# One-token attention over 16 heads on one core: the loads of K and V in another order, two K loads cut in two, and the bookkeeping of a turn moved

## The chip, the core and the metric

The kernel runs on one core of a Trainium2 chip. The core has five engines with queues of their own: PE (TensorE, matrix products; its weight loads are shown as PEld), DVE (VectorE), ACT (ScalarE), POOL (GpSimd) and SP (SyncE, which here only issues transfers). Sixteen DMA engines move data between the chip's main memory and the core's own. The metric is the time of one execution on the device, in microseconds (us).

## The reference

```
B, H, Sq, Sk, D = 1, 16, 1, 8192, 256            # bfloat16
scores = jnp.einsum("bhqd,bhkd->bhqk", q, k) * D ** -0.5
p = _softmax(scores, axis=-1)
return jnp.einsum("bhqk,bhkd->bhqd", p, v)
```

For each of 16 heads there is one query row. It meets 8192 rows of K, the 8192 scores go through a softmax, and the result weighs 8192 rows of V. K and V together are 134 MB, and each byte is used once.

## The kernel before, in words

**Tiling.** The 8192 rows of a head lie on 128 partitions, 64 rows on each: "column" j means the j-th row of each partition, 256 numbers long. One load brings all 64 columns of one head's K or V, 4 MB. K(h) goes to half h mod 2 of `kbuf`, V(h) to `vbuf[h % 2]`, so there are two buffers for each.

**Loads.** SP issues all loads in the order of the string `ORDER`, on one queue. K(h), from h = 2 on, waits until the maximum `m` of head h-2 is done, since then its buffer is free; V(h) waits until PE has finished the products of head h-2 (semaphore `pr`). SP takes its list strictly in order: a load that waits holds all those behind it. A few loads are cut by columns (`V_CUTS`), so that work on the first columns can begin before the rest has landed.

**A turn** is the work for one head's scores. For 24 of the 64 columns POOL multiplies K with q (`prod`, L171, six instructions of four columns each) and ACT sums each of them up (L360). For the other 40 columns DVE does both in one instruction each (L192), in five chunks of eight. All 64 sums per partition are in `S`. Then:

- DVE takes the maximum over the columns (`m`, L207), PE transposes it (L225), DVE takes the maximum over partitions (`g`, L209), PE broadcasts it (L227), ACT negates it (`negb`, L320) and takes the exponential (`E`, L323), whose sum over the columns is `lsum`.
- PE adds `lsum` over the partitions (`total`, L231), and DVE takes the reciprocal (L184).
- PE multiplies the weights `E` with V, two columns at a time in two strips (`doubles`, L238, 32 instructions per head), into the rows of `acc`. ACT copies four part rows of it into `comb` (`collect`, L336), PE adds them up with a selector (`gather`, L250), and ACT scales the row by the reciprocal (`final`, L342).
- The q row of the head after next is cast by PE (L215) and copied by ACT (`q_now`, L314).

The products with V run two heads behind the scores, the collecting and scaling three and four heads behind.

**The order on the engines** is that of the program text: each engine runs a hardware loop over the heads. On PE the turn h is: total of head h-1, products of head h-2, transposed maximum, broadcast, q row, gather. ACT's turn is: exponential of head h-1, six groups of four sums with `q_now` and `final` after the second group, and `collect` at the end. ACT's `collect` in a turn waits for PE's gather of the same turn (`pv`), and the exponential of the next turn stands behind it on ACT's queue.

**The end.** The last head's V lands in six pieces. The first 44 columns go by pairs, the other 20 singly into a row of their own, `ob_last` (L297). After ten of them the last total and the last gather come in.

Of the kernel before, what the change touches and what calls it, by code (L numbers as in the profile page):

```python
# [21 lines left out]
AHEAD = {"k1": 16, "sp": 2, "pr": 2, "cm": 3, "pv": 4, "fin": 4, "rc": 4, "l": 1, "ex": 1, "bc": 1, "nb": 1}  # L22
STREAM_AHEAD = ("v0", "v1", "v0_1", "v1_1", "v1_2")


def bass_standalone__mha_softmax__decode_kernel(nc: bass.Bass, q: bass.AP, k: bass.AP, v: bass.AP, out: bass.AP):
# [17 lines left out]
    def load(kind, h):  # L44
        cuts = (V_CUTS.get(h, (0,)) if kind == "v" else (0,)) + (J,)
        for n, (a, b) in enumerate(zip(cuts, cuts[1:])):
            stream.append((kind, h, a, b, f"{kind}{h % 2}" + (f"_{n}" if n else "")))
# [4 lines left out]
    with contextlib.ExitStack() as ctx:  # L52

        def sb(name, shape, d):
            return ctx.enter_context(nc.sbuf_tensor(name, shape, d))
# [25 lines left out]
        E = sb("E", [P, 2 * EW], BF16)  # L81
        comb = sb("comb", [ROWS, 2 * D], FP32)
        sel = sb("sel", [ROWS, 2], FP32)
# [29 lines left out]
        @(lambda f: f(nc.sync))  # L113
        def _(sp):
            for kind, h, a, b, name in stream:
                if h >= 2 and a == 0:
                    sp.wait_ge(sem("m"), h - 1) if kind == "k" else sp.wait_ge(sem("pr"), h + 1)
                buf = kbuf[:, h % 2 * J * D :] if kind == "k" else vbuf[h % 2]
                sp.dma_start(buf[:, a * D : b * D], src(k if kind == "k" else v, h)[:, a * D : b * D]).then_inc(
                    sem(name), 16  # L120
                )
# [13 lines left out]
        def _(pool):  # L135
# [29 lines left out]
            with pool.Fori(0, H) as h:  # L165
                par = pool.snap(h % 2)
                with pool.Fori(0, NG // 2) as i:
                    k_waits(pool, h)
                    for b in range(2):
                        pool.wait_ge(sem("sp"), h * NG + i * 2 + (b + 1))  # L170
                        pool.tensor_tensor(  # L171
                            out=prod[:, b * GRP * D : (b + 1) * GRP * D].rearrange("p (b d) -> p b d", b=GRP),
                            in0=kbuf[:, ds(par * (J * D) + i * (2 * GRP * D) + (JD + b * GRP) * D, GRP * D)].rearrange(
                                "p (b d) -> p b d", b=GRP
# [6 lines left out]
        def _(dve):  # L181
# [4 lines left out]
            with dve.Fori(0, H) as h:  # L186
                par = dve.snap(h % 2)
                with dve.Fori(0, NC) as c:
                    k_waits(dve, h)
                    for b in range(CH):  # L190
                        col = kbuf[:, ds(par * (J * D) + c * (CH * D) + b * D, D)]
                        ins = dve.scalar_tensor_tensor(  # L192
# [5 lines left out]
                            op1=ALU.mult,  # L198
                            accum_out=S[:, ds(h * J + c * CH + b, 1)],
# [9 lines left out]
                dve.tensor_reduce(g[:, :], mx[0:1, 0:P], AX.X, ALU.max).then_inc(sem("g"), 1)  # L209
            recips(LAST, 0)  # L210

        @(lambda f: f(nc.tensor))
        def _(pe):
# [8 lines left out]

            def maximum(h):
                pe.wait_ge(sem("m"), h + 1)
                pe.matmul(mx[0:1, 0:P], lhsT=m[:, :], rhs=ident[:, :], start=True, stop=True).then_inc(sem("mT"), 1)  # L225
                pe.wait_ge(sem("g"), h + 1)
                pe.matmul(sm, lhsT=ones_row[:, :], rhs=g[:, :], start=True, stop=True).then_inc(sem("bc"), 1)  # L227

            def total(h):
                pe.wait_ge(sem("ex"), h + 1)  # L230
                pe.matmul(tot[0:1, :], lhsT=lsum[:, :], rhs=ones_col[:, :], start=True, stop=True).then_inc(sem("l"), 1)  # L231

# [14 lines left out]

            def gather(dst, first, last):
                for n in range(2):
                    ins = pe.matmul(  # L250
                        dst[0:1, 0:D],
                        lhsT=sel[:, n : n + 1],
                        rhs=comb[:, n * D : (n + 1) * D],
                        start=first and n == 0,
                        stop=last and n == 1,
# [6 lines left out]
            for n in range(2):  # L262
                qcast(n, slice(n, n + 1))
            pe.wait_ge(sem("cf"), 4)
            with pe.Fori(0, H + 2) as h:
                par = pe.snap(h % 2)
                here = pe.snap(h // 2 * 16 + 16)
                late = pe.snap(h // H * 16 + 16)
                with pe.If(h > 0):
                    with pe.If(h < H):  # L270
                        total(h)
                with pe.If(h > 1):
                    with pe.If(par == 0):
                        doubles(0, 0, J, {0: (sem("v0"), here), HALF: (sem("v0_1"), late)}).then_inc(sem("pr"), 1)
                    with pe.If(par == 1):
                        cuts = V_CUTS[LAST]
                        waits = {b: (sem(f"v1_{n}"), late) for n, b in enumerate(cuts) if 0 < b < LAST_PAIRED}
                        doubles(1, 0, LAST_PAIRED, {0: (sem("v1"), here)} | waits)
                        with pe.If(h < H + 1):
                            doubles(1, LAST_PAIRED, J, {}).then_inc(sem("pr"), 1)  # L280
                with pe.If(h < H):
                    maximum(h)
                    qcast(par, ds(h + 2, 1))
                with pe.If(h > 2):
                    pe.wait_ge(sem("cm"), h + 1)
                    pe.wait_ge(sem("fin"), h + 1)
                    gather(ob, True, True).then_inc(sem("pv"), 1)
            for j in range(LAST_PAIRED, J):
                if j in cuts:
                    n = cuts.index(j)  # L290
                    pe.wait_ge(sem(f"v1_{n}"), 32 if f"v1_{n}" in STREAM_AHEAD else 16)
                if j == LAST_PAIRED + GATHER_AFTER:
                    total(H)
                    pe.wait_ge(sem("cm"), H + 3)
                    gather(ob_last, False, False)
                at = EW + j % 2 * HALF + j // 2
# [3 lines left out]
                    rhs=vbuf[1][:, j * D : (j + 1) * D],  # L300
                    start=(j == LAST_PAIRED),
                    stop=(j == J - 1),
                    skip_group_check=True,
                )
                if j == LAST_PAIRED:
                    ins.then_inc(sem("pr"), 1)
            ins.then_inc(sem("pv"), 1)

        @(lambda f: f(nc.scalar))
        def _(act):  # L310
# [21 lines left out]
            def collect(h, n):  # L332
                act.wait_ge(sem("pr"), h - n + 3)
                act.wait_ge(sem("pv"), h - n + 4)
                at = back(h, n) % 2 * (2 * D)
                act.activation(out=comb[:, :], in_=acc[0:ROWS, ds(at, 2 * D)], func=ACT.Copy).then_inc(sem("cm"), 1)  # L336

# [13 lines left out]
            q_copy(0)  # L351
            with act.Fori(0, H) as h:
                with act.If(h > 0):
                    expo(h, 1)
                with act.Fori(0, NG // 2) as i:
                    for n in range(2):
                        act.wait_ge(sem("tp"), h * NG + i * 2 + (n + 1))
                        for b in range(GRP):
                            part = prod[:, (n * GRP + b) * D : (n * GRP + b + 1) * D]
                            ins = act.activation(  # L360
                                out=part,
                                in_=part,
                                func=ACT.Copy,
                                scale=SCALE,
                                accum_out=S[:, ds(h * J + i * (2 * GRP) + (JD + n * GRP + b), 1)],
                            )
                        ins.then_inc(sem("sp"), 1)
# [6 lines left out]
            expo(H - 1, 0)  # L374
            final(H - 4, 0)
            collect(H - 2, 0)
            final(H - 3, 0)
            collect(H - 1, 0)
            final(H - 2, 0)
            final(H - 1, 0, ob_last)  # L380
            act.nop()
# [28 lines left out]
```

## Time and profile before

| what | value |
|---|---|
| median of 3 runs | 321.34 us (321.33 to 321.76) |
| the profiled execution's own time | 321.44 us |
| its span, first to last instruction | 319.8 us |
| mean granted TensorE clock | 0.733 of full speed |
| busy: PE / DVE / ACT / POOL | 42% / 73% / 60% / 64% of the span |
| DMA | 134.26 MB, 420 GB/s over the span |

Busy shares of engines are averages over the whole span. The DMA row of the 40 slices and the chain of the work that ended last say more here: the chain is followed back from the last instruction, at each step to what released it. An SP row is a transfer's issue; "DMA kbuf<-in_k_dram" in the chain is the time from issue to landing. Dates are us from the span's start.

### The profile page before, as it was taken

The numbers are of one execution on the slowest core, as the hardware profiler recorded it, in microseconds if no ns is written. First come the engines' busy times: TensorE is split into PE (matmuls) and PEld (weight loads), VectorE is DVE, ScalarE is ACT, GpSimd is POOL, SyncE is SP. The second block draws the span as 40 slices with busy tenths as digits, with TensorE's granted clock in tenths as the row PEclk, the third lists the DMA queues.
The fourth block names the chain that finished last, engine by engine and source line by source line (L and its number), as shares of the span: only waits on it lengthen the run. The fifth ranks groups of instructions, "written<-read, shape, count | busy, mean of one in ns | idle before, by whom it ended". The sixth has DMA issues, their size and how long they took to land.

```text
span 319.8 us, 7090 instructions
## 1 busy us (share of the span) xinstructions
PE 135.7 (42%) x700; PEld 54.2 (17%) x700; DVE 234.8 (73%) x1328; ACT 192.6 (60%) x866; POOL 203.7 (64%) x112
## 2 busy tenths in 40 slices
PE   0001017070554627264463523646526072370796
PEld 0000003030221212021121211212112030120343
DVE  0296979879795959779595978969695885949700
ACT  2085848666374857757484866747485773757631
POOL 2299785676594893939578575858484874929500
PEclk9999999758575775758576595755758568586799
DMA  8999999999999999999999999999999999999994
GB/s 329 434 418 459 393 455 434 422 451 402 455 422 365 434 418 447 422 439 447 410 447 422 439 434 422 447 410 451 426 430 443 410 451 422 434 434 414 428 410 162
DMA packets 5510, 134.26 MB, mean 420 GB/s; under 512 B 626, under 2 KB 643, under 8 KB 1284
## 3 DMA queue, kind: packets, MB, share of 16 engines
q1 hardware_dynamic: 5476, 134.23, 98.0%
q8 instruction: 1, 0.02, 0.0%
q10 hardware_dynamic: 32, 0.01, 0.0%
q14 instruction: 1, 0.01, 0.0%
HBM read 134.23 MB, written 0.01 MB: 420 GB/s over the span
## 4 chain that ended last, share of the span: by engine, by line
DMA 28%; POOL 23%; issue 13%; PE 12%; DVE 7%; ACT 7%; POOLq 4%; DVEq 3%; ACTq 3%; SPq 0%
POOL prod L171 23%; DMA kbuf<-in_k_dram 14%; DMA vbuf<-in_v_dram 13%; ACT prod L360 6%; DVE kbuf L192 5%; PE ob L250 5%; PE acc L238 2%; PE mx L225 2%; DVEq L192 2%; POOLq L171 2%; PE mx L227 1%; ACTq L360 1%; DVE m L207 1%; DVE g L209 1%; PE ob_last L297 1%
## 5 line engine op out<-in xcount | busy, mean ns | idle before, releaser
L171 POOL TENSOR_TENSOR prod<-kbuf,q_now 128x1024 f32 x96 | 201.8, 2123 | 94.5 <-DMA kbuf<-in_k_dram 46.6
L192 DVE SCALAR_TENSOR_TENSOR kbuf<-kbuf,qrow x640 | 225.0, 417 | 43.8 <-DMA kbuf<-in_k_dram 24.7
L360 ACT ACTIVATE prod<-prod 128x256 f32<-128x256 f32 x384 | 154.7, 404 | 48.3 <-POOL prod L171 48.3
L238 PE MATMUL acc<-vbuf,E 128*64 128x512 bf16 x502 | 86.7, 520 | 44.6 <-DMA vbuf<-in_v_dram 41.6
L360 ACT ACTIVATION_READ_ACCUMULATOR prod<-prod x384 | 71.7, 187 | 0.0
L192 DVE DVE_READ_ACCUMULATOR kbuf<-kbuf,qrow x640 | 52.8, 82 | 0.0
L238 PEld LDWEIGHTS acc<-vbuf,E 128*64 128x64 bf16 x502 | 37.1, 147 | 88.9 <-DMA vbuf<-in_v_dram 43.3
L225 PE MATMUL mx<-ident,m 128*1 128x128 f32 x32 | 8.3, 357 | 102.3 <-DVE m L207 102.1
L336 ACT ACTIVATE comb<-acc 97x512 f32 (+1 forms) x16 | 9.5, 596 | 58.2 <-PE ob L250 54.4
L250 PE MATMUL ob<-comb,sel 97*1 97x256 f32 x60 | 22.9, 524 | 0.4
L225 PEld LDWEIGHTS mx<-ident,m 128*1 128x1 f32 x32 | 1.4, 81 | 109.6 <-DVE m L207 109.6
L207 DVE TENSOR_REDUCE m<-S 128x1 f32 x16 | 3.5, 220 | 15.4 <-ACT prod L360 14.6
L231 PE MATMUL mx<-ones_col,lsum 128*1 128x1 f32 x32 | 3.0, 164 | 23.5 <-ACT E L323 23.5
L209 DVE TENSOR_REDUCE g<-mx 1x1 f32<-1x128 f32 x16 | 4.5, 278 | 9.8 <-PE mx L225 9.8
L184 DVE RECIPROCAL recip<-mx 1x1 f32 (+1 forms) x16 | 2.4, 151 | 12.6 <-PE mx L231 12.6
L323 ACT ACTIVATE E<-S,negb (+1 forms) x16 | 9.3, 580 | 3.9 <-ACT negb L320 3.9
L227 PE MATMUL mx<-g,ones_row 1*128 1x1 f32 x32 | 8.5, 332 | 5.9 <-DVE g L209 5.9
L227 PEld LDWEIGHTS mx<-g,ones_row 1*128 1x128 f32 x32 | 7.1, 276 | 12.9 <-DVE g L209 12.9
L215 PE MATMUL qrow<-q_sb,identb 16*128 16x256 bf16 x18 | 6.1, 350 | 5.7 <-DMA q_sb<-in_q_dram 5.7
L314 ACT ACTIVATE q_now<-qrow (+1 forms) x17 | 6.1, 362 | 3.7 <-PE qrow L215 3.7
L320 ACT ACTIVATE negb<-mx 128x1 f32<-128x1 f32 x16 | 2.6, 165 | 8.7 <-PE mx L227 8.7
L231 PEld LDWEIGHTS mx<-ones_col,lsum 128*1 128x1 f32 x32 | 1.5, 81 | 34.3 <-ACT E L323 34.3
(23 smaller groups left out, 30.3 us busy)
## 6 DMA issues: line engine op xcount, KB each, us to landing
kbuf<-in_k_dram SPq DMA_DIRECT2D x16, 4096.0 KB, 17.4
vbuf<-in_v_dram SPq DMA_DIRECT2D x14, 4096.0 KB, 25.9
vbuf<-in_v_dram SPq DMA_DIRECT2D x2, 2048.0 KB, 20.1
vbuf<-in_v_dram SPq DMA_DIRECT2D x1, 1536.0 KB, 8.2
vbuf<-in_v_dram SPq DMA_DIRECT2D x1, 768.0 KB, 10.5
vbuf<-in_v_dram SPq DMA_DIRECT2D x1, 640.0 KB, 11.6
vbuf<-in_v_dram SPq DMA_DIRECT2D x1, 512.0 KB, 9.1
vbuf<-in_v_dram SPq DMA_DIRECT2D x1, 384.0 KB, 12.1
```

What stands on the lines that cost most here:

```text
L171: pool.tensor_tensor(out=prod[:, b * GRP * D : (b + 1) * GRP * D].rearrange("p (b d) -> p b d", b=GRP), in0=kbuf[:, ds(par * (J * D) + i * ...
L192: ins = dve.scalar_tensor_tensor(out=col, in0=col, scalar=SCALE, in1=qrow[:, ds(par * 512, D)], op0=ALU.mult, op1=ALU.mult, accum_out=S[:, ...
L207: dve.tensor_reduce(m[:, :], S[:, ds(h * J, J)], AX.X, ALU.max).then_inc(sem("m"), 1)
L209: dve.tensor_reduce(g[:, :], mx[0:1, 0:P], AX.X, ALU.max).then_inc(sem("g"), 1)
L215: pe.matmul(qrow[:, ds(at * 512, D)], lhsT=identb[0:H, col].to_broadcast([H, P]), rhs=q_sb[:, :], start=True, stop=True,).then_inc(sem("qp ...
L225: pe.matmul(mx[0:1, 0:P], lhsT=m[:, :], rhs=ident[:, :], start=True, stop=True).then_inc(sem("mT"), 1)
L227: pe.matmul(sm, lhsT=ones_row[:, :], rhs=g[:, :], start=True, stop=True).then_inc(sem("bc"), 1)
L238: ins = pe.matmul(acc[at : at + STRIP, par * 2 * D : (par + 1) * 2 * D], lhsT=E[:, par * EW + j // 2 :][:, 0:STRIP], rhs=vbuf[par][:, j * ...
L250: ins = pe.matmul(dst[0:1, 0:D], lhsT=sel[:, n : n + 1], rhs=comb[:, n * D : (n + 1) * D], start=first and n == 0, stop=last and n == 1, s ...
L323: act.activation(out=E[:, ds(i % 2 * EW, J)].rearrange("p (two x) -> p x two", two=2), in_=S[:, ds(i * J, J)].rearrange("p (x two) -> p x ...
L336: act.activation(out=comb[:, :], in_=acc[0:ROWS, ds(at, 2 * D)], func=ACT.Copy).then_inc(sem("cm"), 1)
L360: ins = act.activation(out=part, in_=part, func=ACT.Copy, scale=SCALE, accum_out=S[:, ds(h * J + i * (2 * GRP) + (JD + n * GRP + b), 1)],)
```

## The change

It has six parts.

1. **Order of loads**: V0 and V1 stand ahead of K2, and V4 ahead of K6; K6 and K7 stand next to each other.
2. **K5 and K15 in two pieces**, columns 0 to 33 and 34 to 63. The second piece has a semaphore of its own (`k1_1`), on which DVE waits before each chunk with a computed value.
3. **GpSimd's 24 columns are the first of a head**, DVE's 40 the last, in four chunks of ten. The reciprocal moves from behind the fourth chunk to behind the second.
4. **Bookkeeping on ACT**: one loop over 19 turns. The part rows (`collect`) of head h-3 are copied at the beginning of turn h, then come the exponential, `final` and the q row, and then the six groups. `comb` has two halves.
5. **Bookkeeping on PE**: the gather stands between the transposed maximum and the broadcast, in each turn; the total is taken in each turn, and the last one ahead of the last gathers.
6. **The end**: 32 columns by pairs, the last 32 singly, added to the row that the last gather begins.

```
-CH = 8
+CH = 10
-V_CUTS = {14: (0, 32), 15: (0, 24, 32, 44, 54, 60)}
-LAST_PAIRED = 44
-GATHER_AFTER = 10
+CUTS = {"k5": (0, 34), "k15": (0, 34), "v14": (0, 32), "v15": (0, 24, 32, 44, 54, 60)}
-ORDER = "k0 k1 v0 k2 v1 k3 v2 k4 v3 k5 k6 v4 k7 v5 k8 ..."
+ORDER = "k0 k1 v0 v1 k2 k3 v2 k4 v3 k5 v4 k6 k7 v5 k8 ..."
+LAST_PAIRED = 32
...
 # SP
-sp.wait_ge(sem("m"), h - 1) if kind == "k" else sp.wait_ge(sem("pr"), h + 1)
+sp.wait_ge(sem("m"), h - 1) if kind == "k" else sp.wait_ge(sem("pr"), h + 2)
...
 # POOL
+pool.memset(lsum[:, :], 0.0).then_inc(sem("cf"), 1)
+pool.memset(comb[:, :], 0.0).then_inc(sem("cf"), 1)
...
 # DVE
+dve.wait_ge(sem("k1_1"), (h * 8 + c + 39) // 80 * 16 + 16)
 for b in range(CH):
-    col = kbuf[:, ds(par * (J * D) + c * (CH * D) + b * D, D)]
+    col = kbuf[:, ds(par * (J * D) + c * (CH * D) + (NPL + b) * D, D)]
...
-with dve.If(c == 3):
+with dve.If(c == 1):
     with dve.If(h > 0):
         recips(h, 1)
...
 # PE, in the loop
 with pe.If(h < H):
-    maximum(h)
-    qcast(par, ds(h + 2, 1))
-with pe.If(h > 2):
-    pe.wait_ge(sem("cm"), h + 1)
-    pe.wait_ge(sem("fin"), h + 1)
-    gather(ob, True, True).then_inc(sem("pv"), 1)
+    pe.wait_ge(sem("m"), h + 1)
+    pe.matmul(mx[0:1, 0:P], lhsT=m[:, :], rhs=ident[:, :], ...).then_inc(sem("mT"), 1)
+pe.wait_ge(sem("cm"), h + 1)
+pe.wait_ge(sem("fin"), h + 1)
+gather(ob, 1 - par, True).then_inc(sem("pv"), 1)
+with pe.If(h < H):
+    pe.wait_ge(sem("g"), h + 1)
+    pe.matmul(sm, lhsT=ones_row[:, :], rhs=g[:, :], ...).then_inc(sem("bc"), 1)
+    qcast(par, ds(h + 2, 1))
...
 # ACT
-with act.Fori(0, H) as h:
-    with act.If(h > 0):
-        expo(h, 1)
-    with act.Fori(0, NG // 2) as i:
-        ...
-        with act.If(i == 0):
-            q_copy(h + 1)
-            with act.If(h > 3):
-                final(h, 4)
-    with act.If(h > 1):
-        collect(h, 2)
+with act.Fori(0, H + 3) as h:
+    with act.If(h > 2):
+        collect(h, 3)
+    with act.If(h > 0):
+        with act.If(h < H + 1):
+            expo(h, 1)
+    with act.If(h > 3):
+        final(h, 4)
+    with act.If(h < H):
+        q_copy(h + 1)
+        with act.Fori(0, NG // 2) as i:
+            ...
```

Three places of the built programs show what moved. The first is SP's queue at its beginning; kbuf and vbuf are the buffers of K and V, `m` a head's maximum, `pr` the products with V. Of the change:

```order
L119 DMA kbuf<-in_k_dram 128x16384 [waits barrier_Pool_Activation_PE_DVE_SP_release]
L119 DMA kbuf<-in_k_dram 128x16384
L119 DMA vbuf<-in_v_dram 128x16384 x2
L119 DMA kbuf<-in_k_dram 128x16384 [waits m] x2
L119 DMA vbuf<-in_v_dram 128x16384 [waits pr]
L119 DMA kbuf<-in_k_dram 128x16384 [waits m]
L119 DMA vbuf<-in_v_dram 128x16384 [waits pr]
L119 DMA kbuf<-in_k_dram 128x8704 [waits m]
L119 DMA kbuf<-in_k_dram 128x7680
L119 DMA vbuf<-in_v_dram 128x16384 [waits pr]
L119 DMA kbuf<-in_k_dram 128x16384 [waits m] x2
```

Before, K2 with its wait stood between V0 and V1, and K5 and K6 followed each other; now the two V loads without a wait come first, K2 and K3 follow each other, and K6 and K7 do.

The second place is PE's turn behind the products: mx holds the transposed maximum, ob the gathered row, comb the part rows. Before:

```order
L225 MATMUL mx<-ident,m 1x128 [waits m]
L227 MATMUL mx<-g,ones_row 128x1 [waits g]
L215 ISA
L215 REGISTER_ALU
L215 MATMUL qrow<-q_sb,identb 128x256
L281 UNCONDITIONAL_BRANCH
L284 COMPARE_AND_BRANCH
L285 REGISTER_ALU
L250 MATMUL ob<-comb,sel 1x256 [waits fin,cm]
L250 MATMUL ob<-comb,sel 1x256
```

Of the change, at the same place:

```order
L281 MATMUL mx<-ident,m 1x128 [waits m]
L279 UNCONDITIONAL_BRANCH
L282 REGISTER_ALU
L248 REGISTER_ALU [waits fin,cm]
L248 ISA
L248 MATMUL ob<-comb,sel 1x256
L248 ISA
L248 MATMUL ob<-comb,sel 1x256
L285 COMPARE_AND_BRANCH
L287 MATMUL mx<-g,ones_row 128x1 [waits g]
```

The two matrix instructions of the gather, which the engine runs as four passes, have moved from behind the broadcast and the q row to ahead of them.

The third place is the beginning of ACT's turn in the change, down to the exponential and what now stands behind it:

```order
L332 ISA [waits pv,pr]
L332 ACTIVATE comb<-acc 97x512
L349 UNCONDITIONAL_BRANCH
L351 COMPARE_AND_BRANCH
L352 COMPARE_AND_BRANCH
L315 REGISTER_ALU
L316 ACTIVATE negb<-mx 128x1 [waits bc]
L319 ISA [waits nb]
```

The copy of the part rows stood at the end of the turn, with a wait for the gather of the same turn. Now it opens the turn, and its `pv` asks for the gather of the turn before the last.

More of the change, by code (lines that the diff above doesn't have):

```diff
@@ L81, in bass_standalone__mha_softmax__decode_kernel @@
         E = sb("E", [P, 2 * EW], BF16)
-        comb = sb("comb", [ROWS, 2 * D], FP32)
+        comb = sb("comb", [ROWS, 2 * 2 * D], FP32)
         sel = sb("sel", [ROWS, 2], FP32)
@@ L209, in _ @@
                 dve.tensor_reduce(g[:, :], mx[0:1, 0:P], AX.X, ALU.max).then_inc(sem("g"), 1)
-            recips(LAST, 0)
+            dve.wait_ge(sem("pr"), LAST + 4)
+            dve.reciprocal(recip[0:1, LAST : LAST + 1], tot[0:1, :]).then_inc(sem("rc"), 1)
         @(lambda f: f(nc.tensor))
@@ L221, in qcast @@
                 ).then_inc(sem("qp"), 1)
[L223 to L227, printed above, removed]
             def total(h):
                 pe.wait_ge(sem("ex"), h + 1)
-                pe.matmul(tot[0:1, :], lhsT=lsum[:, :], rhs=ones_col[:, :], start=True, stop=True).then_inc(sem("l"), 1)
+                return pe.matmul(tot[0:1, :], lhsT=lsum[:, :], rhs=ones_col[:, :], start=True, stop=True)
             def doubles(par, a, b, waits):
@@ L246, in doubles, with gather @@
                 return ins
-            def gather(dst, first, last):
+            def gather(dst, at, last):
                 for n in range(2):
@@ L252, in gather @@
                         lhsT=sel[:, n : n + 1],
-                        rhs=comb[:, n * D : (n + 1) * D],
-                        start=first and n == 0,
+                        rhs=comb[:, ds(at * (2 * D) + n * D, D)],
+                        start=n == 0,
                         stop=last and n == 1,
@@ L263, in _ @@
                 qcast(n, slice(n, n + 1))
[L264 removed]
+            pe.wait_ge(sem("cf"), 6)
+            cuts = CUTS[f"v{LAST}"]
             with pe.Fori(0, H + 2) as h:
@@ L300, in _ @@
                     rhs=vbuf[1][:, j * D : (j + 1) * D],
-                    start=(j == LAST_PAIRED),
+                    start=False,
                     stop=(j == J - 1),
@@ L332, in collect @@
             def collect(h, n):
[L333 to L336, printed above, removed]
+                act.wait_ge(sem("pr"), h - n + 4)
+                act.wait_ge(sem("pv"), h - n + 3)
+                at = ds(back(h, n) % 2 * (2 * D), 2 * D)
+                act.activation(out=comb[:, at], in_=acc[0:ROWS, at], func=ACT.Copy).then_inc(sem("cm"), 1)
             def final(h, n, rows=ob):
@@ L374, in _ @@
[L374 to L380, printed above, removed]
+                    with act.If(h < H + 1):
[5 more added lines that the diff above has]
+                    with act.Fori(0, NG // 2) as i:
+                        for n in range(2):
+                            act.wait_ge(sem("tp"), h * NG + i * 2 + (n + 1))
+                            for b in range(GRP):
+                                part = prod[:, (n * GRP + b) * D : (n * GRP + b + 1) * D]
+                                ins = act.activation(
+                                    out=part,
+                                    in_=part,
+                                    func=ACT.Copy,
+                                    scale=SCALE,
+                                    accum_out=S[:, ds(back(h, 0) * J + i * (2 * GRP) + (n * GRP + b), 1)],
+                                )
+                            ins.then_inc(sem("sp"), 1)
@@ L381, in _ @@
+            final(LAST, 0, ob_last)
             act.nop()
```

47 lines of the change are left out of this document (16 added, 31 removed).

## The prediction

> **What bounds the kernel now.** I read the page's 40 slices first, then the chain that ended last for the dates of transfers, then SP's own queue in order of time.
>
> ```profile
> DMA  8999999999999999999999999999999999999994
> GB/s 329 434 418 459 393 455 434 422 451 402 455 422 365 434 418 447 422 439 447 410 447 422 439 434 422 447 410 451 426 430 443 410 451 422 434 434 414 428 410 162
> ```
>
> The DMA engines are busy in every slice: every byte of K and V is read once, on one queue, so the end is the last landing plus the work behind it. Only three things can move it: time in which the queue is empty, time that a packet takes, and the tail. The chain gives the price of one load (4 MB, 64 columns); a row is issue time and time to landing:
>
> ```profile
> 0.74 12.24 DMA kbuf<-in_k_dram
> ...
> 29.24 13.21 DMA kbuf<-in_k_dram
> ...
> 227.41 20.48 DMA kbuf<-in_k_dram
> ...
> 264.41 32.04 DMA vbuf<-in_v_dram
> ...
> 296.49 5.23 PE acc L238 x32
> ...
> 302.59 10.49 DMA vbuf<-in_v_dram
> ```
>
> The transfers are K0 (landed 12.98), K2 (42.45), K13 (247.89), V13 (296.45) and columns 32 to 43 of V15 (313.08); the PE row is V13's product. From K13 to V13 are five loads in 48.56 us: 9.71 us each with a full queue. With that step I date every other load. K0 to K2 is three loads: 29.14 expected, 29.47 measured, 0.33 lost. K2 to K13 is 21 loads: 203.95 expected, 205.44 measured, 1.49 lost. The slice of 365 GB/s tells where; in windows of 4 us (start:end, length, busy time of PE, PEld, DVE, ACT, POOL, granted clock, DMA share, GB/s):
>
> ```profile
> 96.00:100.00 4.00, 0.59 (x2) 0.09 (x2) 1.96 (x12) 2.51 (x13) 0.97 (x1) 0.50 0.74 320
> 100.00:104.00 4.00, 2.61 (x7) 0.87 (x7) 2.81 (x16) 0.77 (x3) 2.66 (x2) 0.50 1.04 385
> ```
>
> Why it runs dry is in SP's queue (start, length, transfers):
>
> ```profile
> 46.45 0.33 SPq L119 DMA_DIRECT2D kbuf<-in_k_dram  x1
> 55.45 0.33 SPq L119 DMA_DIRECT2D vbuf<-in_v_dram  x1
> 63.67 0.33 SPq L119 DMA_DIRECT2D kbuf<-in_k_dram  x1
> 72.69 0.33 SPq L119 DMA_DIRECT2D vbuf<-in_v_dram  x1
> 80.88 18.64 SPq L119 DMA_DIRECT2D kbuf<-in_k_dram  x2
> 99.56 0.43 SPq L119 DMA_DIRECT2D vbuf<-in_v_dram  x1
> 117.50 0.33 SPq L119 DMA_DIRECT2D kbuf<-in_k_dram  x1
> ```
>
> K(h+2) is issued when head h's maximum `m` is done, so the K rows date the heads: K3 46.45, K4 63.67, K5 80.88, K6 99.19 (the end of the merged row less 0.33), K7 117.50. A turn is 17.2 us for heads 1 to 3 and 18.3 for heads 4 and 5. I call "lead" the time from an issue to the landing of the load ahead of it. K2 had 3.16 (V0 lands at 32.40) and lost 0.33; K6 had 1.53 (K5 lands at 100.72) and lost 1.5; K7 had 4.1 and lost nothing. A load into an empty queue lands 12.24 (K0) to 12.73 us (K6) after its issue. So a load needs some 4 us of lead, and below 1.5 its landing is its issue plus 12.7.
>
> **The change, part by part.**
>
> *Order of loads.* V1 needs no wait, so K2 now stands behind a full queue: its 0.33 goes. But K2 lands at 12.98 + 4 x 9.71 = 51.8, not 42.45, and head 1 is done at about 46.2: head 2 now waits for its data. From K0's landing to K2's issue were 29.24 - 12.98 = 16.26 us, so K4 is issued at 68.1. V2 lands at 71.2 (two loads behind K2), a lead of 3.1: 0.33 lost again, K4 lands at 81.3. V3 waits for head 1's products on PE; before they ended 72.69 - 63.67 = 9.0 us after K4's issue, now some 1.2 later because of the gather (below): 78.3, a lead of 3.0, about 0.4 lost (0 to 0.9). V3 lands at 91.4, K5 (two pieces) at 101.2, V4 at 110.9, K6 at 120.6. K6 is issued at about 103, far ahead: its 1.5 us goes. K7 then stands right behind K6 and waits for head 5's `m`, three turns after head 2's: 68.1 + 3 turns.
>
> *The turn.* This is the number that decides. Heads 2 and 3 of the kernel before had no gather ahead of them; head 4 had one, and its turn of 18.3 reads (PE, then ACT):
>
> ```profile
> 99.22 0.59 PE L225 MATMUL mx<-ident,m 128*1 128x128 f32 x2 [6.53 <-DVE m L207]
> 100.18 0.58 PE L227 MATMUL mx<-g,ones_row 1*128 1x1 f32 x2 [0.37 <-DVE g L209]
> 100.63 0.37 PE L215 MATMUL qrow<-q_sb,identb 16*128 16x256 bf16 x1
> 100.93 1.87 PE L250 MATMUL ob<-comb,sel 97*1 97x256 f32 x4
> ```
>
> ```profile
> 102.98 0.60 ACT L336 ACTIVATE comb<-acc 97x512 f32 x1 [4.19 <-PE ob L250]
> 103.47 0.16 ACT L320 ACTIVATE negb<-mx 128x1 f32<-128x1 f32 x1
> 103.89 0.58 ACT L323 ACTIVATE E<-S,negb  x1 [0.26 <-ACT negb L320]
> ```
>
> ACT copies the part rows (comb) only when the gather is over, and the exponential stands behind that. The change copies them at the beginning of ACT's turn, beside the wait for `m`: that takes 0.5 us off the path. The gather moves ahead of the broadcast (L227). Its four passes step by about 0.45 (1.87 in all, 0.50 of the clock in both windows above), so the broadcast begins 0.58 (L225) + 1.8 after 99.22, at about 101.5, and ends at 102.1; negb follows at 102.1 instead of 103.47, 1.4 us earlier. Against that, `q_now` and `o_all` now stand ahead of the first prod of the turn:
>
> ```profile
> L342 ACT ACTIVATE o_all<-ob,recip 1x256 f32 (+1 forms) x15 | 6.7, 449 | 0.0
> L314 ACT ACTIVATE q_now<-qrow (+1 forms) x17 | 6.1, 362 | 3.7 <-PE qrow L215 3.7
> ```
>
> 0.45 + 0.36 = 0.81, no longer hidden behind POOL. Net -0.6: the ACT side of the turn is 18.3 - 0.6 = 17.7 (17.3 for head 3, which has no `o_all` yet). The DVE side was 17.2 where no gather stood. There the change drops one of five chunk beginnings and adds a register step with a wait to each; the row nearest to it is the beginning of a head:
>
> ```profile
> 48.55 0.42 DVE L192 SCALAR_TENSOR_TENSOR kbuf<-kbuf,qrow  x1 [1.16 <-issue]
> ```
>
> One step of several within 1.16 us is 0.2 to 0.3; I leave DVE at 17.2 (17.0 to 17.5). So the three turns are 17.3 + 17.6 + 17.5 = 52.4, between 51.3 (DVE alone) and 54.9 (nothing gained).
>
> *K7.* Issued at 68.1 + 52.4 = 120.5, with K6 landing at 120.6: the queue is empty. It lands at 120.5 + 12.7 = 133.2. Before: 42.45 + 9 x 9.71 + 1.49 = 131.3. K7 is the thirteenth load in both orders, so everything behind it is 1.9 us later, unless another wait comes; V5 behind it lands at 142.9, K8 is issued a turn after K7, at 138: a lead of nearly 5 us, and each later turn gains on the DMA's 19.4 per head.
>
> *K5 and K15 in two pieces, GpSimd on the first columns.* GpSimd's 24 and DVE's first ten columns lie in the first piece, so a head can begin 30/64 x 9.71 = 4.6 us earlier, if it waits for K. Head 5 does not: head 4 ends at 103, K5 lands at 101.2. Head 15 does, but the next thing on PE is V13's product, which ends at 301.7 with or without it. Gain nothing; price: from V13 to the 302.59 row's landing are 16.63 us for 108 columns, 16.39 at the full rate, so five pieces cost 0.24, 0.05 a piece. K15's two pieces are +0.1; K5's lie ahead of K7's wait and cost nothing. The Trainium skill, "DMA: Bandwidth & Descriptors", section on the anatomy of one DMA, speaks against cutting: about 2.0 us fixed for each transfer, which for K15 alone would make the sum an estimated 1.9 us higher. This trace disagrees for transfers queued behind one another (0.05 us), and I go by it.
>
> *GpSimd's two more memsets* lie under its wait for K0:
>
> ```profile
> POOL prod L171 <- DMA kbuf<-in_k_dram: 46.6, 11, 9.3
> ```
>
> The longest, 9.3 us, is that one: the two would have to take that long together to be seen.
>
> *The tail.* PE works through it without a pause that lasts:
>
> ```profile
> 313.12 0.84 PE L238 MATMUL acc<-vbuf,E 128*64 128x512 bf16 x6 [0.99 <-DMA vbuf<-in_v_dram]
> 314.00 1.02 PE L250 MATMUL ob<-comb,sel 97*1 97x256 f32 x4
> 314.86 1.26 PE L297 MATMUL ob_last<-vbuf,E 128*1 128x256 bf16 x10
> 315.95 0.19 PE L231 MATMUL mx<-ones_col,lsum 128*1 128x1 f32 x2
> 316.01 1.02 PE L250 MATMUL ob_last<-comb,sel 97*1 97x256 f32 x4
> 316.87 1.26 PE L297 MATMUL ob_last<-vbuf,E 128*1 128x256 bf16 x10
> ```
>
> A single column steps by 1.09/10 = 0.109, a gather takes 0.86; the last column begins to count at 316.87 + 1.09 = 317.96. The last landing is 313.08 + 20/64 x 9.71 + 3 x 0.05 = 316.3, so PE is 1.3 us behind the data there. On the same clock the change has its four last pairs at 311.2 (columns 24 to 31), then 0.9 to the gather (as 313.12 to 314.00), two gathers 1.7 with ACT's copy (0.60) beside the first, and 32 singles 3.5: 317.4. Gain 0.5; at most 1.3 (data), at least -0.1 (copy not hidden).
>
> *Sum.* Profiled execution 321.44 (span 319.8, the rest lies around it): +1.9 (K7) + 0.1 - 0.5 = +1.5, 322.9. The median of the runs is 0.1 lower: 322.8, slower by 0.5%.
>
> **Rivals.**
> 1. *K7 comes in time* (faster). If three turns took 48.9 or less (16.3 each), K7 would be issued at 117.0, 3.6 us ahead, lose next to nothing and land at 130.3: -1.0 + 0.1 - 0.5, 320.0. For it: the early copy does shorten ACT's side. Against: DVE alone stood at 17.2. Break-even is a turn of about 17.0.
> 2. *No change*: a turn of 16.6 to 17.1, or more of the tail's 1.3: 320.7 to 321.9.
> 3. *The turn stays 18.3*, as the gather ahead of the broadcast and DVE's register steps eat what the early copy gives: K7 issued at 123.0, landing 135.7, +4.4 + 0.1 - 0.5: 325.3.
> 4. *A cut transfer costs as an empty queue does*: K15's second piece 1.5 us as K6's did: 324.2. No row here speaks for it, the five pieces of V14 and V15 against it. This is what the rule of the skill's page named above comes to.
>
> **How the numbers follow.** My forecast (turns of 17.1 to 17.9; alone 321.7 to 324.1) 0.60, rival 1 0.15, rival 2 0.11, rival 3 0.12, rival 4 0.02. A measurement of this kernel tells about 0.2% (0.64 us) from no change. Faster: rival 1 and a little of 2, 0.17. Same: the rest of 2 and the lower edge of the forecast, 0.17. Slower: 0.66. The range 320.3 to 324.6 leaves out half of rival 1 and rival 3.
>
> **What would show it.** Right: SP issues K4 near 68, K7 near 120.5; GB/s is even at 96 to 104 and dips at 120 to 124; POOL and DVE wait for K2 until 51.8; collect (comb) starts right behind ACT's last prod; the chain ends with 32 single columns in a row on PE. Wrong: K issues less than 17.0 us apart from K4 on, no dip near 120, or a new dip elsewhere, say at V3 (81).

## The result and the profile after

The changed kernel took 323.76 us (median of 4 runs, 323.51 to 324.07), the kernel before 321.47 (4 runs, 321.33 to 321.76) on the same chip: ratio 1.0070, 95% interval 1.0053 to 1.0088. It is slower by 2.3 us. The forecast was 322.8 in a range of 320.3 to 324.6. The profiled execution took 323.62 us, its span is 321.5.

The 40 slices of the changed kernel:

```profile
DMA  8999999999999988999999999999999999999994
GB/s 327 436 412 457 432 416 457 400 428 428 424 424 445 432 347 351 432 448 404 453 436 412 453 424 428 448 404 453 432 416 453 416 436 440 411 449 412 428 411 192
```

The dip of the kernel before (365 in the slice from 96 to 104) is gone; a wider one stands two slices on, 347 and 351 between 112 and 128. In windows of 4 us, with the columns as before:

```profile
116.00:120.00 4.00, 0.00 (x0) 0.00 (x0) 3.81 (x22) 3.01 (x15) 2.58 (x2) 0.61 0.71 303
120.00:124.00 4.00, 3.13 (x9) 0.96 (x9) 1.31 (x7) 1.05 (x5) 2.24 (x2) 0.50 0.72 238
124.00:128.00 4.00, 2.87 (x16) 1.33 (x18) 3.90 (x23) 3.78 (x17) 2.45 (x2) 0.50 0.97 418
```

The rate falls before K6, the last load in the queue, has landed (121.02), and is back to its height only behind 124. SP's queue gives the dates (start, length, transfers):

```profile
29.08 17.82 SPq L119 DMA_DIRECT2D kbuf<-in_k_dram  x2
56.88 0.33 SPq L119 DMA_DIRECT2D vbuf<-in_v_dram  x1
67.94 0.33 SPq L119 DMA_DIRECT2D kbuf<-in_k_dram  x1
77.94 0.33 SPq L119 DMA_DIRECT2D vbuf<-in_v_dram  x1
85.42 0.80 SPq L119 DMA_DIRECT2D kbuf<-in_k_dram  x2
...
103.11 18.02 SPq L119 DMA_DIRECT2D kbuf<-in_k_dram  x2
...
138.45 0.33 SPq L119 DMA_DIRECT2D kbuf<-in_k_dram  x1
```

The first row holds K2 and K3, the one at 103.11 K6 and K7; K7 is issued at the end of that row less its own 0.33, at 120.80. The rows of one K load date K4 (67.94), K5 (85.42, in two pieces) and K8 (138.45). So K4, K5, K6, K7 and K8 are 17.48, 17.69, 17.69 and 17.65 us apart: that is the turn now.

Out of the chain that ended last (start, length), for the dates of K2, K6, V13, the bookkeeping of a turn, and the end:

```profile
29.08 22.69 DMA kbuf<-in_k_dram
...
103.11 17.91 DMA kbuf<-in_k_dram
...
138.48 0.59 PE mx L281 x2
139.06 1.80 PE ob L248 x4
140.86 0.53 PE mx L287 x2
...
266.61 31.74 DMA vbuf<-in_v_dram
...
311.87 1.92 PE acc L236 x16
...
314.36 1.02 PE ob L248 x4
315.38 0.86 PE ob_last L248 x4
316.25 3.51 PE ob_last L295 x32
```

K2 lands at 51.77, 9.3 us later than before. V13 lands at 298.35, before at 264.41 + 32.04 = 296.45: 1.90 later. V13's landing lies behind every place at which the queue can run short and ahead of the tail, so I use it below as a ruler: before is 0, the change +1.90.

Load by load, from issue and landing, a load loses what its landing lies beyond the landing ahead of it plus 9.71. Three groups of SP's transfers in the changed kernel, each of one load (V2, K4, K7), with issue and time to landing:

```profile
L119 SPq DMA_DIRECT2D vbuf<-in_v_dram x1: 328/328/328, 56.9 to 56.9; - x1
...
DMA to landing us min/median/max: 14.3/14.3/14.3
```

```profile
L119 SPq DMA_DIRECT2D kbuf<-in_k_dram x1: 327/327/327, 67.9 to 67.9; - x1
...
DMA to landing us min/median/max: 14.2/14.2/14.2
```

```profile
L119 SPq DMA_DIRECT2D kbuf<-in_k_dram x1: 328/328/328, 120.8 to 120.8; - x1
...
DMA to landing us min/median/max: 12.2/12.2/12.2
```

V2 lands at 71.19, K4 at 82.10: 10.91 instead of 9.71, 1.2 lost at a lead of 3.25. K7 lands at 132.99, 2.26 lost at a lead of 0.22. K8 lost 0.20 (lead 4.22), V3 0.01 (lead 4.16). With the 0.08 that K5 takes longer in two pieces these are 3.75, the kernel before lost 1.84: the difference, 1.91, is the 1.90 of V13.

### The profile page after: what moved, and what is told of

It is laid out like the page before. It is cut to its first block, busy times and chain, and to the rows that moved or that the text cites. A ratio compares the mean times of both kernels' runs of the same rounds, so it can differ in the third digit from the quotient of the medians.

```text
span 321.5 us, 7154 instructions
## 1 busy us (share of the span) xinstructions
PE 139.3 (43%) x720; PEld 55.6 (17%) x720; DVE 233.4 (73%) x1328; ACT 194.3 (60%) x866; POOL 204.7 (64%) x114
## 4 chain that ended last, share of the span: by engine, by line
DMA 42%; POOL 24%; issue 10%; PE 8%; ACT 6%; POOLq 4%; ACTq 3%; DVE 1%; SPq 0%; DVEq 0%
DMA kbuf<-in_k_dram 30%; POOL prod L173 24%; DMA vbuf<-in_v_dram 12%; ACT prod L363 6%; PE ob L248 3%; PE acc L236 2%; POOLq L173 2%; ACTq L363 1%; PE ob_last L295 1%; PE mx L281 1%; POOLq L172 1%; PE mx L287 1%; DVE m L210 1%; POOLq L169 1%; ACTq L358 0%
## 5 line engine op out<-in xcount | busy, mean ns | idle before, releaser
L248 PE MATMUL ob<-comb,sel 97*1 x72 | 27.7, 526 | 1.2 <-issue 0.8
L332 ACT ACTIVATE comb<-acc x16 | 9.3, 583 | 9.5 <-PE acc L236 7.2
L319 ACT ACTIVATE E<-S,negb x16 | 9.3, 579 | 4.2 <-ACT negb L316 4.2
L248 PEld LDWEIGHTS ob<-comb,sel 97*1 97x1 f32 x72 | 5.6, 95 | 16.0 <-issue 14.1
L338 ACT ACTIVATE o_all<-ob,recip 1x256 f32 x15 | 7.0, 465 | 1.3 <-PE ob L248 1.3
```

Of the source, the lines that this page charges most:

```text
L248: ins = pe.matmul(dst[0:1, 0:D], lhsT=sel[:, n : n + 1], rhs=comb[:, ds(at * (2 * D) + n * D, D)], start=n == 0, stop=last and n == 1, ski ...
L319: act.activation(out=E[:, ds(i % 2 * EW, J)].rearrange("p (two x) -> p x two", two=2), in_=S[:, ds(i * J, J)].rearrange("p (x two) -> p x ...
L332: act.activation(out=comb[:, at], in_=acc[0:ROWS, at], func=ACT.Copy).then_inc(sem("cm"), 1)
L338: act.activation(out=o_all[:, ds(i * D, D)], in_=rows[0:1, 0:D], func=ACT.Copy, scale=recip[0:1, ds(i, 1)],).then_inc(sem("fin"), 1)
```

## Experiments

Two questions were open behind the result: which part of the change costs, and where the half microsecond comes from that is not in the span (323.62 - 321.5 = 2.1 us outside it, before 321.44 - 319.8 = 1.6). The table has all runs; "span" is the median over the runs of a kernel, "V13" the landing of V13 in its profile against the kernel before, "outside" the time less the span over all runs. One execution of each kernel was profiled, and it is not always near the median: the profiled spans of e1 (319.2), e6 (323.0) and e7 (321.3) are ends of their scatter, and those of e4 (323.6) and e9 (323.4) lie 2 us above their medians, which is why their V13 stands in brackets. The kernel before, run beside them, had spans of 319.5 to 324.3, median 320.0, and 1.51 to 1.73 outside. Those spans scatter more than the three runs known at the forecast showed.

| kernel | time, us | ratio (95%) | span | V13 | outside |
|---|---|---|---|---|---|
| the change | 323.76 | 1.0070 (1.0053 to 1.0088) | 321.45 | +1.90 | 2.1 to 2.7 |
| its order undone (e1) | 322.76 | 1.0033 (1.0004 to 1.0061) | 320.4 | -0.41 | 2.1 to 2.7 |
| order alone (e2) | 324.70 | 1.0080 (1.0043 to 1.0117) | 323.0 | +3.19 | 1.6 to 1.7 |
| K and V by turns (e3) | 331.52 | 1.0304 (1.0260 to 1.0347) | 328.9 | -1.54 | 2.2 to 2.8 |
| loads uncut (e4) | 323.27 | 1.0040 (1.0019 to 1.0061) | 321.6 | (+3.92) | 1.7 |
| only V4 ahead (e5) | 322.44 | 1.0011 (0.9985 to 1.0037) | 320.1 | -0.01 | 2.1 to 2.7 |
| only V1 ahead (e6) | 325.81 | 1.0112 (1.0070 to 1.0154) | 323.5 | +3.41 | 2.1 to 2.5 |
| only V4 ahead, uncut (e7) | 322.02 | 1.0000 (0.9976 to 1.0024) | 320.2 | +1.60 | 1.7 to 1.8 |
| one more semaphore (e8) | 322.09 | 0.9999 (0.9967 to 1.0030) | 320.3 | +0.35 | 1.7 to 1.8 |
| the wait alone (e9) | 324.00 | 1.0061 (1.0026 to 1.0097) | 321.4 | (+3.79) | 2.1 to 2.6 |
| two small transfers (e10) | 323.34 | 1.0052 (1.0014 to 1.0089) | 321.6 | +1.89 | 1.7 to 1.8 |
| K0 and K6 cut (e11) | 320.04 | 0.9946 (0.9915 to 0.9977) | 318.1 | -1.56 | 1.9 to 2.1 |
| K0 cut (e12) | 320.01 | 0.9938 (0.9908 to 0.9968) | 318.3 | -1.46 | 1.7 to 1.8 |

**e1: the change with the order of loads of before.**

```
-ORDER = "k0 k1 v0 v1 k2 k3 v2 k4 v3 k5 v4 k6 k7 v5 ..."
+ORDER = "k0 k1 v0 k2 v1 k3 v2 k4 v3 k5 k6 v4 k7 v5 ..."
```

> The changed kernel with the order of loads of the kernel before; everything else (cuts, columns, bookkeeping, tail) stays changed. Theory A (the new order loses: K2 lands 9.4 us later, head 2 waits for it, K7 is issued into an empty queue): K2 is issued at 29.1, K3 46.6, K4 64.1, K5 81.7, K6 99.3 with K5 landing at 100.8 (1.5 us lost), K7 117.0 with 4.8 us of lead (nothing lost). K7 lands at 131.5 instead of 133.0; span 320.0, time 322.2. Theory B (the moved bookkeeping or the cuts lose, the order is neutral): span stays at 321.5, time 323.8.

SP's queue and V13's row of the chain:

```profile
64.15 0.33 SPq L118 DMA_DIRECT2D kbuf<-in_k_dram  x1
74.28 0.33 SPq L118 DMA_DIRECT2D vbuf<-in_v_dram  x1
81.62 18.03 SPq L118 DMA_DIRECT2D kbuf<-in_k_dram  x3
99.69 0.43 SPq L118 DMA_DIRECT2D vbuf<-in_v_dram  x1
117.00 0.33 SPq L118 DMA_DIRECT2D kbuf<-in_k_dram  x1
```

```profile
264.31 31.73 DMA vbuf<-in_v_dram
```

K4 is issued 3.8 us earlier than in the change, K7 at 117.00, 4.1 us ahead of the landing of V4, which stands before it in this order, and loses 0.03. V13 lands at 296.04. So the order is what costs in the span: undone, it takes 1.0 off the median span, and 2.3 off V13's landing in the profile, which is the shortest of ten runs with spans of 319.2 to 322.1. Theory A had expected a span of 320.0, near the median of 320.4, but 1.5 lost at K6, which lost 0.51 with a lead of 1.85. The time stays 0.9 above the kernel before, and about two thirds of that lie outside the span.

**e2: the kernel before with the new order and nothing else.** The diff is the one above with the signs exchanged.

> The kernel before with nothing but the new order of loads. Theory A: head 2 waits for K2 until 51.8, K4 is issued at 68.1, then turns of 17.2, 18.3, 18.3, so K7 at 121.9 into an empty queue, landing at 134.4 (131.3 before); span 322.9, time 324.5. Theory B: span stays at 319.8 or falls by the 1.5 us of K6's stall, time 320 to 321.5.

```profile
103.68 18.64 SPq L119 DMA_DIRECT2D kbuf<-in_k_dram  x2
```

```profile
268.44 31.20 DMA vbuf<-in_v_dram
```

K7 is issued at 103.68 + 18.64 - 0.33 = 121.99 and lands at 134.20, 3.14 lost. The expectation was 121.9, 134.4 and a span of 322.9; measured 323.0. So the order alone costs 3 us. The other parts of the change issue K7 1.2 earlier (120.80), by turns of 17.69 instead of 18.31 from head 4 on. That the bookkeeping on PE and ACT shortens the turn is argued from the rows: no run undoes the bookkeeping, the choice of columns and the tail one by one.

**e5 and e6: one of the two moved V loads each.** In e5 V1 goes back behind K2 and V4 stays ahead of K6, in e6 the other way round.

```
 e5: "k0 k1 v0 k2 v1 k3 v2 k4 v3 k5 v4 k6 k7 v5 ..."
 e6: "k0 k1 v0 v1 k2 k3 v2 k4 v3 k5 k6 v4 k7 v5 ..."
```

> The changed kernel with V1 behind K2 again; V4 stays ahead of K6. Theory A, made sharper (it is V1 ahead of K2 that loses, by the 4.5 us that head 2 waits for K2; V4 ahead of K6 is harmless or a gain): K2 issued at 29.1 (0.3 to 0.6 lost), K4 64.1, K5 81.6, K6 99.3 with 11 us of lead, K7 117.0 with K6 landing at 120.6, a lead of 3.6 (0.2 to 1.2 lost). K7 lands at 130.5 to 131.5 instead of 133.0; span 318.8 to 319.8. Rival (V4 ahead of K6, which puts K6 and K7 side by side, loses by itself): K7 lands at 132 or later, span 321 or more.

> The changed kernel with K6 ahead of V4 again; V1 stays ahead of K2. Theory A: K6 is issued at 103.1 with K5 landed at 101.6, so the queue is empty and K6 lands at 115.8 (4.4 us lost); V4 lands at 125.5, K7, issued at 120.8, has a lead of 4.7 and lands at 135.2; span 323.7. Rival (the loss hangs on V4 ahead of K6): span 320 to 321.

V13's row of e5, then of e6, and windows of 2 us of e6:

```profile
264.71 31.73 DMA vbuf<-in_v_dram
```

```profile
268.11 31.75 DMA vbuf<-in_v_dram
```

```profile
98.00:100.00 2.00, 0.00 (x0) 0.00 (x0) 1.90 (x11) 1.22 (x7) 2.00 (x2) 1.00 0.85 361
100.00:102.00 2.00, 0.00 (x0) 0.00 (x0) 2.00 (x13) 1.70 (x9) 1.71 (x2) 0.73 0.13 54
102.00:104.00 2.00, 0.90 (x3) 0.17 (x4) 0.69 (x4) 1.15 (x5) 2.00 (x2) 0.50 0.00 0
104.00:106.00 2.00, 2.00 (x7) 0.78 (x5) 0.54 (x3) 0.00 (x0) 1.33 (x1) 0.50 1.06 328
```

With V1 alone ahead, K6 is issued at 103.07, 0.4 us after K5 has landed, and the DMA engines all but stand still from 100 to 104 (shares 0.13 and 0.00). K6 loses 2.86, K4 1.34, V3 0.95. This is the 323.7 that was expected (spans of 323.0 to 324.0). With V4 alone ahead nothing waits that way, but K2 lost 1.36 with 3.24 us of lead where 0.3 to 0.6 was expected, and the spans of e5 run from 319.0 to 321.2 instead of 318.8 to 319.8. The four orders on otherwise the same kernel, by median span: neither 320.4, V4 320.1, V1 323.5, both 321.45. So V1 ahead of K2 costs 3.1 without the other move and 1.3 with it, and V4 ahead of K6 repays 2.0 of V1's cost; by itself it brings 0.3, less than the scatter.

**e3: K and V strictly by turns**, V1 behind K2, down to K14 and K15, which stand together; K13 is the one cut.

```
 ORDER = "k0 k1 v0 k2 v1 k3 v2 k4 v3 k5 v4 k6 v5 k7 v6 k8 ... k13 v12 k14 k15 v13 v14 v15"
 CUTS: k13 at 34 instead of k5 and k15
```

> The changed kernel with another order: V1 behind K2 again, then K and V strictly by turns to the end (k5 v4 k6 v5 k7 v6 ...), so that no two K loads stand next to each other until K14 and K15; K13 instead of K5 and K15 is cut in two, so that K15 has lead. Theory A: only K2 loses (0.33 us); K7 has 13 us of lead. Last landing about 314.7, span 318.0, time 320.2, below both kernels. Theory B: the order is neutral, span 321.5. A third outcome, if a V load now comes too late for PE or K15 for the last head: a dip in GB/s behind 240 us and a span over 319.

A miss: 328.7 in the profile, not 318.0. The first half of the thought held: the queue hardly runs dry (K2 loses 0.18, the first piece of V15 0.66), and the last byte lands at 315.34, 0.9 earlier than before. But K14 stands one load later in the queue and lands at 275.48. From its chain (start, length):

```profile
291.40 0.23 DVE m L209
...
309.05 0.23 DVE m L209
...
312.45 6.22 PE acc L235 x32
...
323.46 3.51 PE ob_last L294 x32
```

Head 14's maximum comes at 291.40, head 15's one turn of 17.65 later, at 309.05, and PE then has all of V14, landed since 304.73, and V15 to work through. So K comes too late for the last heads, an outcome that the expectation named, though without the dip in GB/s that it expected to see there. A queue that is always full is not enough: K must run far enough ahead that the last two turns end with the last landing.

**e4: the change with K5 and K15 whole**, without the semaphore and DVE's wait for it.

```
-CUTS = {"k5": (0, 34), "k15": (0, 34), "v14": (0, 32), ...}
+CUTS = {"v14": (0, 32), ...}
-dve.wait_ge(sem("k1_1"), (h * 8 + c + 39) // 80 * 16 + 16)
```

> The changed kernel with K5 and K15 whole again and without DVE's wait for the second piece. Theory A: K5's cut is hidden behind K7's wait, K15's costs 0.1 us, and ACT sets the turn, so DVE's register step is free: span 321.4, time 323.6 to 323.8. Rival (the cuts or DVE's step carry the loss): the K issues come closer than 17.6 us from K5 on and the span falls by 1 us or more. It also tells whether the 0.5 us that the change added outside the span hangs on the cuts: then the time falls by 0.5 more than the span.

The median span is 321.6, that of the change 321.45: the cuts neither cost nor bring anything there. But the time outside the span is back at 1.7. (The profiled run was the longest of its eleven, 323.6, so its loads are only used further down.)

**e7: e5 and e4 together**: V1 behind K2, V4 ahead of K6, nothing of K cut.

> As e5 (V1 behind K2, V4 ahead of K6), with K5 and K15 whole and without the semaphore and DVE's wait for a second piece. Theory A: span 0.2 below that of e5, 318.6 to 319.6. If the 0.5 to 1.0 us that the runs with cut K loads spend outside the span hang on the cuts, the time is span plus 1.7, 320.3 to 321.3, the lowest so far; if not, span plus 2.2.

The spans run from 318.5 to 321.3: the expected 318.6 to 319.6 was the lower end of it only. The profiled run, one of the two longest of ten, lost 1.10 at K2 and 2.00 at K7, with leads of 3.23 and 3.38 us; this is what led to e11 and e12.

**e8, e9, e10: what lies outside the span.** The cut of K5 and K15 brings a semaphore, a wait with a computed value in DVE's loop, and two more transfers. e8 is the kernel before with one more semaphore that nothing uses. e9 is e4 with the semaphore and the wait, whose value is always met. e10 is e4 with two small loads into a spare buffer.

```
 e8:  +STREAM_AHEAD = ("k1_1", "v0", "v1", ...)
 e9:  +dve.wait_ge(sem("k1_1"), (h * 8 + c + 39) // 800 * 16 + 16)
 e10: +if (kind, h) in (("k", 5), ("k", 15)):
      +    sp.dma_start(spare[:, at : at + 64], src(k, h)[:, 0:64]).then_inc(sem("k1_1"), 16)
```

> The kernel before with one more semaphore (raised once by GpSimd at the beginning, never waited for). In the runs so far the time exceeds the span by 1.6 to 1.8 us in kernels without the semaphore of the second K piece and by 2.1 to 2.8 in those with it. Theory S (one semaphore more costs that, at the beginning or the end): time minus span 2.1 to 2.8 here. Rival (DVE's computed wait, or the two more transfers): 1.6 to 1.8. The span stays at 319.8 in both.

> The changed kernel with K5 and K15 whole, but DVE's computed wait at each chunk kept, with a value that is always met. In whole-K runs the time exceeded the span by 1.67 to 1.84 us, in runs with cut K loads by 2.08 to 2.67, and one more semaphore alone gave 1.69 to 1.82. Theory W (the computed wait, a longer program, costs it): 2.1 or more here. Rival T (two more transfers): 1.65 to 1.85. The span stays at 321.3 to 321.9 in both.

> The changed kernel with K5 and K15 whole and without DVE's wait, but with two more small transfers (128 rows of 64 numbers into a spare buffer that nothing reads) on a semaphore of their own behind K5 and K15. Theory T (two more transfers cost the time outside the span): 2.1 or more. Rival W: 1.65 to 1.85. Span 321.3 to 322.2.

Outside the span lie 1.69 to 1.82 us in e8, 1.69 to 1.77 in e10, and 2.13 to 2.62 in e9. So it is the wait with a computed value: against e4 (1.67 to 1.75) it adds 0.4 to 0.9 us that no row of the profile shows. A semaphore accounts for some 0.15 at most by the medians (1.73 in e8, 1.59 in the kernel before), and e4 has 1.72 without it; the transfers account for nothing. The other kernels with a computed wait lie above those without (the change, e1, e5, e6 2.1 to 2.7; e3 2.2 to 2.8; e11 1.9 to 2.1, the least). e12, whose wait is for a constant, has 1.67 to 1.84. No run separates the wait from the register steps that work out its value, and how it lengthens the time ahead of the first or behind the last instruction is not settled.

**e11 and e12: K0 cut, so that K2 gets its lead.** Both are e7 with K0 in two pieces, so that head 0 begins on the first 34 columns. e11 cuts K6 too, with a computed wait; e12 has the cut of K0 alone, and DVE waits for a constant.

```
 e11: +CUTS = {"k0": (0, 34), "k6": (0, 34), ...}
      +if b == CH - 1:
      +    dve.wait_ge(sem("k0_1"), (h * 4 + c + 40) // 64 * 16 + 16)
 e12: +CUTS = {"k0": (0, 34), ...}
      +dve.wait_ge(sem("k0_1"), 16)     # behind the instructions of a chunk
```

> The changed kernel with loads in the order of e7 (V1 behind K2, V4 ahead of K6), and instead of K5 and K15 the loads K0 and K6 cut in two at column 34; DVE waits for the second pieces ahead of the tenth column of a chunk. Theory A (every load needs some 4 us of lead; a lead of 3.2 costs 0.2 to 2 us by chance): head 0 begins 4.5 us earlier, K2 is issued at 25 with 7 us of lead, K7 at 113 with 7, K8 at 132 with 7, no load below 5. All loads land 9.72 us apart; last landing 314.6, span 318.0 in all runs within 0.3 us, against 319.5 to 322.4 of the kernel before. Rival (the queue loses 1 to 2 us somewhere whatever the lead): span 319 or more, and spread as before.

> As e11 with K0 cut alone, and a constant wait. Theory A: K2 has 7 us of lead, K7 7 us, but K8 waits for head 6, which now waits for the whole of K6: issued at 136.3 with V5 landing at 139.5, a lead of 3.2. So all loads but K8 land 9.72 apart, K8 loses 0.2 to 2 us, and the spans spread over 318.2 to 320.

POOL's first work, SP's K2 and V1, and V13's row of e12:

```profile
9.20 4.20 POOL L172 TENSOR_TENSOR prod<-kbuf,q_now 128x1024 f32 x2 [3.99 <-DMA kbuf<-in_k_dram]
```

```profile
25.46 0.33 SPq L118 DMA_DIRECT2D kbuf<-in_k_dram  x1
25.83 0.43 SPq L118 DMA_DIRECT2D vbuf<-in_v_dram  x1
```

```profile
262.86 32.13 DMA vbuf<-in_v_dram
```

K2 is issued at 25.46 instead of 29.24, 7.0 us ahead of V0's landing, and loses nothing; V13 lands 1.46 earlier than before, near the 1.6 that this kernel saves (it lost 0.07 at K7 and 0.18 at K8, against 1.84). Ten of e12's twelve spans lie between 317.9 and 318.8. In e11 the span of 318.0 came as expected in eleven of twelve runs (317.9 to 318.2; the twelfth took 320.4), but not by way of K6: in both kernels K7 was expected to have 7 us of lead and had 3.44 and 3.36, since head 5, a turn after K5's landing, still sets its date. Cutting K6 brought nothing that e12 does not have. Both are faster than the kernel before, by 0.5 and 0.6%; e12 is the version that I would keep.

## Why the prediction was right

**The cause** stood as it was put: head 2 waits for K2, and K7 comes into an empty queue three turns later. The forecast dates were 51.8 for K2's landing (51.77), 68.1 for K4's issue (67.94), 120.5 for K7's (120.80), 120.6 for K6's landing (121.02), 133.2 for K7's (132.99). DVE's first step on K2:

```profile
52.81 0.42 DVE L195 SCALAR_TENSOR_TENSOR kbuf<-kbuf,qrow  x1 [5.31 <-issue]
```

**The turn** was 17.48, 17.69 and 17.69, forecast 17.3, 17.6 and 17.5: ACT's side of 17.7 was the one that held. The copy of the part rows does stand right behind the last sum of a turn:

```profile
67.36 0.18 ACT L363 ACTIVATION_READ_ACCUMULATOR prod<-prod  x1
67.45 0.57 ACT L332 ACTIVATE comb<-acc  x1
```

and the gather's 1.80 between transposed maximum and broadcast (the chain above) took what the prediction gave it. Rival 1 needed a turn of 16.3 and rival 3 one of 18.3. e2, which keeps the old bookkeeping, comes nearest to rival 3, though the first of its three turns is 17.21 and only the other two are 18.31: with 324.70 it came 0.6 below the 325.3 of that rival.

**K7's landing** came out within 0.2 by errors that cancelled, and that was luck. The three turns took 52.86 instead of 52.4 and K7 was issued 0.3 late; an empty queue was put at 12.7 us from issue to landing and took 12.2. K7 is then only 1.66 later than before, not 1.9. That V13 is 1.90 later all the same comes from K8 above all, whose 0.20 the prediction had put at nothing.

The step that failed is the reading of a loss as a function of the lead, from three loads of one trace: K4's loss was put at 0.33 and was 1.2, V3's at 0.4 and was 0.01. It did not matter in this profile, since K7's date goes by the heads and not by K4's landing; in e10, where K4 lost 1.71, K7 lands at 133.02. But it can matter. In the two long profiles, e4 and e9, V3 lost 1.58 and 1.35 as well, and K7, issued at the same 120.8 with leads of 1.81 and 1.69, landed at 135.2 and 135.1, two us later than in the change. K7 of e4:

```profile
L119 SPq DMA_DIRECT2D kbuf<-in_k_dram x1: 327/327/327, 120.8 to 120.8; - x1
...
DMA to landing us min/median/max: 14.5/14.5/14.5
```

**The cuts.** 0.05 a piece was right: K5 took 9.79 and K15 9.79 in two pieces where a whole load takes 9.71. Rival 4 is refuted by this and by e4, whose uncut loads do not shorten the span. The Trainium skill, "DMA: Bandwidth & Descriptors", section on the anatomy of one DMA, counts about 2.0 us fixed for a transfer, measured there on transfers that GpSimd issues. This trace, with transfers that SP issues and that stand behind others in the queue, does not show such a cost: K15 in two pieces took 0.08 longer than a whole load.

**GpSimd's memsets** stayed under the wait for K0, which is 0.9 us shorter at its longest (9.3 before) and still there:

```profile
POOL prod L173 <- DMA kbuf<-in_k_dram: 30.6, 9, 8.4
```

**The tail** gained 0.3, not 0.5. PE ends at 316.25 + 3.51 = 319.76, before at 316.87 + 1.26 = 318.13, 1.63 later, and the last landing (318.18) is 1.92 later. The total of the last head now stands ahead of the gather: from the products' end (313.79) to the gather's start are 0.57, where before there were 0.04. That was not in the sum.

**What the sum had no term for** is the 0.5 us outside the span. The span went up by 1.7 against a forecast of 1.5; the time by 2.3, since DVE's computed wait costs 0.4 to 0.9 outside (e9). The sum took the rest around the span to be the same for both kernels. The prediction priced that wait by its steps within a turn, where it costs nothing that shows.

## What to carry to other kernels

In a kernel bound by one queue of large loads, date each load's issue and the landing of the load ahead; moving a load that waits for nothing ahead of one that is needed soon fills the queue now and starves the engines a few turns later, which comes back as a late issue further on. With loads like these, give each waiting load 4 us of lead or more; at 3.0 to 3.5 us its loss was anything from 0 to 2 us, and one profile with a small loss there is no measure of it. Compare the time with the span: if the difference between the two changes from one kernel to the next, its cause lies in neither an engine's nor a queue's rows.

## What the runs showed of the hardware

**Loss and lead.** The 4 MB loads of all profiles in which the queue came near its end:

| lead, us | lost, us |
|---|---|
| 4.0 to 5.0 | 0 to 0.04, once 0.20 (K8 of the change) |
| 3.6 to 3.7 | 0.34, 0.95 |
| 3.0 to 3.5 | 0 to 0.07 (four loads), 0.18 to 0.55 (five), 1.1 to 2.0 (twelve) |
| 1.5 to 1.9 | 0.5, 1.5, 2.9, 2.9 |
| 0.7 and less | 1.7 to 3.1; issue to landing 12.2 |

The third row was the surprise. K2 of e7 and of the kernel before have leads of 3.23 and 3.16, and lost 1.10 and 0.34; K2 and K6 of e8, in one execution, lost 1.95 and 0.01 with 3.15 each. K7 of e7 with 3.38 lost 2.00, nearly what K7 of the change lost with 0.22. K4, on the other hand, lost 1.2 to 1.7 in each of the six kernels with V1 ahead, with leads of 3.16 to 3.26. And a lead of 3.4 need not cost: K7 and K8 of e12, with 3.36 and 3.31, lost 0.07 and 0.18.

The start and length of single packets tell more. In e6, at the end of K5, 16 packets are under way at 99.50, 7 at 100.00, 2 at 101.00, one until 102.36; the landing is 102.67. So the engines end the same load up to 2.5 us apart, and the landing goes by the last. K6, issued at 103.07, has its first packet at 104.03, 1.0 us after. By these figures a load with a lead of 3.2 us, counted to the landing, has its packets some 2 us ahead of it, which would be too late for an engine that ends earlier than that. The counts of packets under way agree: at K7 of e7 (lost 2.00) 10 of 16 at 119.25 and 15 until 121.75, at K4 of the change (lost 1.2) 13 at 70.50 and 14 at 71.25, at K7 of e12 (lost 0.07) 15 at 119.25 alone.

A pause is not all of it. The first packets of such a load also take longer: up to 2.57 us at K4 of the change, where a packet in a full queue takes 1.21 to 1.22. At K2 of e8 one packet is missing for 0.75 us, and the packet that follows takes 2.49; together that is 2.0 us beyond the usual, and 1.95 were lost. At K2 of the kernel before no packet is missing, packets take up to 1.53, and 0.34 were lost. The records carry no engine's number, so that a single late engine makes up the whole loss is a reading of these rows, not shown. Which engine is late, and why it differs from kernel to kernel, stays open. Nor was it shown, for want of several profiles of one kernel, that this is what makes the spans of the kernel before scatter (its K2 has such a lead) and those of e12 narrow (its K2 has 7 us).

**Time outside the span** is not the same for all kernels: 1.5 to 1.8 us, or 1.9 to 2.8 with a computed wait in DVE's loop; e9 shows that this wait, with the steps that work out its value, is the cause.
